# A different order of loads and of some twenty operations in the opening of a one-core attention and feed-forward kernel

## The chip, the cores and the metric

One core of a Trainium2 chip runs the program. The metric is the device time of one execution in microseconds (us); of several executions the median is taken.

## What is computed

Attention with a band and block summaries, then a feed-forward layer with a softmax-gated activation and a normalization. The reference, cut to what matters (4 batches, 8 heads, 768 positions, 64 wide; `d_model` 512, `d_ff` 1024):

```python
k_sum = k.reshape(B, H, nb, 32, D).max(axis=3)
v_sum = v.reshape(B, H, nb, 32, D).mean(axis=3)
scores_l = where(abs(i - j) < 16, scale * q @ k.T, -1e9)
scores_s = scale * q @ k_sum.T + log(32)
a = softmax(concatenate([scores_l, scores_s], -1))
x = a @ concatenate([v, v_sum])
h = x @ w_in
solu = h * softmax(h)
ln = (solu - mean) / sqrt(var + 1e-6) * g_ln
out = ln @ w_out
```

## The kernel before

**Tiling.** Queries are taken in groups of 256 positions (three per batch). For half of the heads of a group there is one round: `scores` (L671) multiplies queries with a window of 96 keys and 24 block maxima, VectorE (DVE) adds the mask and takes maxima, ScalarE (ACT) makes exponentials, a multiplication by the reciprocal sum follows (DVE or GpSimd, POOL), `values_turn` (L762) transposes the result on TensorE (PE), two copies bring it to SBUF, and `values` (L773) multiplies it with the value rows. The block means of `v` are rows 96 to 119 of that product: for batch 0 `mean_values_first` (L581) makes them on PE from three row blocks, for batch 1 `mean_values_pe` (L597) from three others. The result is split into a high and a low part (`xh`, `xl`), and `first` (L948) multiplies 128 rows with `w_in`, three matmuls per piece of weights (high by low, low by high, high by high). `solu` (L1023) does the gate and the normalization, `turn` (L1119) transposes, `second` (L1137) multiplies with `w_out`. Both weight matrices arrive as 64-bit words and are turned into two 32-bit parts by `rounded` (L487) and `split_w_in` or `split_w_out` (L522, L528): scale, sign bits, low word, shift, add, round (high part), subtract (low part), spread over ACT, DVE and POOL.

**Order.** Every call of `op` makes an operation that has a number, the engines that can run it, a planned cost and dependencies. `order` (L292) simulates a greedy schedule; `move` (L238) then takes each entry `(operation, engine, after)` of `MOVES` (L118), removes the operation from where it was and puts it behind the named one in that engine's line. `issue` (L210) emits the result: each engine runs its line in order. While PE's planned time is below `FILL` (L97), `keep_up` (L366) puts fillers, matmuls on zeros (L1346), ahead of the next PE operation.

**Loads.** Nearly all are issued by SyncE (SP, the queue's own rows are SPq) in one line; a few by ACT. Eight completion semaphores are used in turn by all loads, so a load is issued when the one eight places ahead of it has landed. In this text:

- w0 to w7 are the 512 KB pieces of `w_in` (w5 is operation 11), w8 to w15 those of `w_out` (w14 is 125, w15 is 126).
- r0, r1, r2 are the 512 KB value row blocks of batch 0 (12, 13, 14), r3, r4, r5 those of batch 1 (115, 116, 117).
- Q1 and Q2 are the 512 KB queries of the second and third group (Q2 is 136), V0, V1, V2 the 1024 KB value windows of the first three groups (V2 is 137).
- SP's order before: w0 k w1 w2 q k k k q w3 w4 w5 r0 r1 r2 V0 w6 w7 g Q1 V1 r3 w8 to w15 r4 r5 Q2 V2 and so on.
- ACT issues the broadcast of the block means into rows 96 to 119 of each value window of batch 0 (`load_v2`, L664): into V1 (114) and into V2 (242), each when that window has landed.

**PE's order in the opening.** Fillers; scores of group 0; 20 fillers; block means from r0 (32) and r1 (33); transpose (53); block means from r2 (34); transpose (73); values (56, 76); scores of group 1 (129); `first(0)` (138 to 145); scores (187); `first(1)` (195 to 202) with a transpose (179) and values (182) inside; block means from r3 and r4 (243); transpose (236); from r5 (244); `first(2)` begins (262); values (239); scores of group 2 (252), which read Q2; and so on.

Of the kernel before, what the change touches and what calls it, by code (L numbers as in the profile page):

```python
# [85 lines left out]
class Plan:  # L86
# [7 lines left out]
    SMALL, LATE = 40.0, 50.0  # L94
    LAND = 2.2
    START = 0.7
    COLD, FILL = 6.9, 21.6  # L97
    IDLE = 0.22
    WAIT, FAR = 1.5, 200
    DEAR = {"dve": 1.0, "act": 0.3, "pool": 1.0}  # L100
# [15 lines left out]


    MOVES = ((53, "pe", 33), (200, "pe", 199), (317, "pe", 327), (308, "pe", 317), (35, "act", 55), (77, "act", 109),  # L118
        (315, "act", 227), (296, "act", 240), (158, "act", 296), (214, "act", 301), (391, "act", 354),
        (247, "act", 380), (249, "act", 383), (526, "act", 446), (540, "act", 547), (602, "act", 582),  # L120
        (613, "act", 612), (664, "act", 668), (679, "act", 672), (1396, "act", 1196), (1875, "act", 1855),
        (102, "dve", 103), (146, "dve", 130), (175, "dve", 147), (171, "dve", 154), (223, "dve", 171),
        (203, "dve", 155), (210, "dve", 209), (297, "dve", 293), (314, "dve", 388), (322, "dve", 314),
        (371, "dve", 364), (527, "dve", 450), (452, "dve", 410), (445, "dve", 442), (419, "dve", 418),
        (663, "dve", 560), (706, "dve", 707), (678, "dve", 660), (869, "dve", 812), (1223, "dve", 1222),
        (1287, "dve", 1224), (1864, "dve", 1874), (97, "pool", 186), (99, "pool", 118), (250, "pool", 251),
        (170, "pool", 113), (233, "pool", 176), (234, "pool", 233), (298, "pool", 163), (213, "pool", 298),
        (420, "pool", 351), (606, "pool", 1150), (561, "pool", 606), (615, "pool", 585), (562, "pool", 615),
        (589, "pool", 588), (680, "pool", 1154), (814, "pool", 1300), (753, "pool", 1302), (909, "pool", 1303),)

    def __init__(self):
        self.ops, self.rings, self.banks, self.idle, self.slots = [], {}, {}, None, []
# [1259 lines left out]
```

## Time and profile before

| | |
|---|---|
| median of 3 runs | 356.59 us (355.8 to 357.35) |
| profiled execution | 356.37 us |
| its span, first to last instruction | 354.6 us |
| PE busy | 349.5 us, 99% |
| DVE, ACT, POOL busy | 294.7, 276.6, 167.2 us |
| chain that ended last | PE 93%, DMA 5% |

Times of rows are counted from the start of the span. Busy times overlap between engines. What the profile calls idle is the time an engine waited right before an instruction; behind the arrow stands what ended it. The DMA share can be a little above 1 because packets overlap.

### The profile page before, as it was taken

The page shows a single profiled execution, that of the slowest core. Times are in us where ns is not written, and L with a number is a line of the kernel's source. Part 1 is how long each engine was busy: PE and PEld are TensorE (multiplying, and loading weights), DVE is VectorE, ACT ScalarE, POOL GpSimd, SP SyncE. Part 2 cuts the span into 40 slices and gives each one's busy share as a digit, 9 for nine tenths or more (in the row PEclk, how much of TensorE's full clock was granted, in tenths as well). Part 3 has the DMA queues.
Part 4 walks back from the last instruction along what each step waited for, and adds up shares of the span by engine and source line. Part 5 has one row for each costly group of instructions (what it writes and reads, how often), then busy time and mean ns, then how long its engine had stood idle before and what let it go on. Part 6 is the DMA issues. An engine that isn't in the chain of part 4 may idle for free.

```text
span 354.6 us, 9335 instructions
## 1 busy us (share of the span) xinstructions
PE 349.5 (99%) x3312; PEld 275.4 (78%) x3312; DVE 294.7 (83%) x946; ACT 276.6 (78%) x810; POOL 167.2 (47%) x301
## 2 busy tenths in 40 slices
PE   8999999999999999999999999999999999999996
PEld 3528767878777887888888888888888888888886
DVE  3898999998999998996899998896897996947431
ACT  5777999997879979799796894994995996946310
POOL 6626425369777998307805445240335053533200
PEclk9999999999999999999999999999999999999999
DMA  7999996054525247267498382573443382344611
GB/s 250 412 408 408 352 411 227 35 129 156 179 84 190 95 150 259 82 212 255 144 284 288 93 274 99 168 259 132 152 153 136 97 283 63 126 142 169 216 61 59
DMA packets 28531, 68.19 MB, mean 192 GB/s; under 512 B 3853, under 2 KB 13325, under 8 KB 26949
## 3 DMA queue, kind: packets, MB, share of 16 engines
q1 hardware_dynamic: 24620, 60.87, 51.3%
q10 hardware_dynamic: 3864, 6.74, 5.3%
q8 instruction: 26, 0.43, 0.5%
q14 instruction: 21, 0.16, 0.1%
HBM read 49.55 MB, written 15.73 MB: 184 GB/s over the span
## 4 chain that ended last, share of the span: by engine, by line
PE 93%; DMA 5%; SPq 0%; ACT 0%; issue 0%; DVE 0%
PE o L1154 38%; PE h L959 13%; PE hu L978 13%; PE x L807 7%; PE hl L978 6%; PE hf L978 3%; DMA st_v<-in_vr 3%; PE s_0l L705 3%; PE s_1l L705 2%; DMA qt<-in_q 2%; PE t_0l L760 2%; PE t_1l L760 2%; PE vs_ps L591 2%; PE vs_ps1l L604 1%; PE x L799 1%; PE s_0r L705 0%
## 5 line engine op out<-in xcount | busy, mean ns | idle before, releaser
L1154 PE MATMUL o<-w,lh 128*128 128x512 f32 (+1 forms) x400 | 127.6, 385 | 0.0
L1154 PEld LDWEIGHTS o<-w,lh 128*128 128x128 f32 x400 | 74.1, 188 | 15.3 <-ACT at L405 0.2
L1154 PE MATMUL o<-w,ll 128*128 128x512 f32 (+1 forms) x200 | 76.2, 381 | 0.0
L732 ACT ACTIVATE e<-e,nm 128x120 f32<-128x120 f32 x192 | 73.4, 392 | 0.0
L959 PE MATMUL h<-w,xh 128*128 128x512 f32 x128 | 43.2, 401 | 0.0
L1154 PEld LDWEIGHTS o<-w,ll 128*128 128x128 f32 x200 | 37.6, 188 | 6.9
L732 ACT ACTIVATION_READ_ACCUMULATOR e<-e,nm 128x1 f32 x192 | 37.9, 197 | 0.0
L959 PEld LDWEIGHTS h<-w,xh 128*128 128x128 f32 x128 | 24.0, 188 | 6.7 <-ACT kw L405 0.8
L413 POOL TENSOR_TENSOR ll<-lt,lh 128x512 fp32r<-128x512 f32 x11 | 16.0, 1465 | 26.2 <-DVE lh L406 19.2
L633 POOL TENSOR_TENSOR st_v<-st_v 96x512 f32<-96x512 f32 (+3 forms) x28 | 23.9, 862 | 8.2 <-DMA st_v<-in_vb 7.7
L807 PEld LDWEIGHTS x<-at,vt 120*64 120x64 f32 (+1 forms) x768 | 24.4, 138 | 4.1 <-issue 2.0
L1061 ACT ACTIVATE he<-he,nmu 128x512 f32<-128x512 f32 x35 | 24.2, 722 | 4.0 <-DVE nmu L1052 3.6
L807 PE MATMUL x<-at,vt 120*64 120x64 f32 (+1 forms) x768 | 26.5, 224 | 0.0
L1064 ACT ACTIVATE sq<-he 128x1024 bf16<-128x1024 f32 x24 | 25.4, 1059 | 0.1
L1084 DVE STREAM_TRANSPOSE tbl<-he 128x1024 f32<-128x1024 f32 x18 | 22.3, 1239 | 3.9 <-ACT he L1061 2.3
L959 PE MATMUL h<-w,xl 128*128 128x512 f32 x64 | 25.0, 390 | 0.0
L1041 ACT ACTIVATE he<-hs,hm 128x512 f32<-128x512 f32 x24 | 17.2, 718 | 9.1 <-DVE hm L1031 9.1
L413 POOL TENSOR_TENSOR cv<-cv 128x512 int32<-128x512 int32 x8 | 11.0, 1378 | 26.2 <-ACT cv L509 13.3
L412 DVE TENSOR_TENSOR e<-e,z 128x960 f32<-128x960 f32 x18 | 22.2, 1232 | 0.1
L1160 ACT ACTIVATE os<-o,y 128x512 f32<-128x512 f32 x19 | 13.0, 685 | 11.7 <-PE o L1154 11.5
L413 POOL TENSOR_TENSOR xl<-sums,xh 128x256 fp32r<-128x256 f32 (+1 forms) x12 | 12.4, 1034 | 19.4 <-ACT xh L405 19.4
L412 DVE TENSOR_TENSOR ll<-lt,lh 128x512 fp32r<-128x512 f32 x25 | 19.7, 804 | 0.5 <-ACT lh L405 0.3
(250 smaller groups left out, 959.8 us busy)
## 6 DMA issues: line engine op xcount, KB each, us to landing
vt<-in_v SPq DMA_DIRECT2D x12, 1024.0 KB
farl<-tbl SPq DMA_DIRECT2D x18, 512.0 KB
lt<-farl SPq DMA_DIRECT2D x72, 128.0 KB
kraw<-in_k SPq DMA_DIRECT2D x16, 400.0 KB
out<-os ACTq DMA_DIRECT2D x23, 256.0 KB
qt<-in_q SPq DMA_DIRECT2D x11, 512.0 KB
raw<-in_w_in SPq DMA_DIRECT2D x8, 512.0 KB
raw<-in_w_out SPq DMA_DIRECT2D x8, 512.0 KB
```

Of the source, the lines that this page charges most:

```text
L412: by = {dve: lambda: nc.vector.tensor_tensor(out=to(), in0=a(), in1=b(), op=kind), pool: lambda: nc.gpsimd.tensor_tensor(out=to(), in0=a() ...
L413: pool: lambda: nc.gpsimd.tensor_tensor(out=to(), in0=a(), in1=b(), op=kind)}
L633: op(pool, 0.15 + w * 0.0021, lambda w=w, o=o: nc.gpsimd.tensor_tensor(out=o.ap[:n, :w], in0=x.ap[:n, :w], in1=x.ap[:n, w:2 * w], op=ALU.add),
L705: nc.tensor.matmul(sc.ap[j][cu * QT:(cu + 1) * QT, c:c + ks.shape[-1]], qs.ap[ds, 2 * pp + i, u * QT:(u + 1) * QT], ks, start=True, stop=True)
L732: nc.scalar.activation(out=e.ap[:, n, :], in_=e.ap[:, n, :], func=AF.Exp, bias=nm.ap[:, n:n + 1], scale=-1.0, accum_out=z.ap[:, n:n + 1])
L807: nc.tensor.matmul(xp()[j * D:(j + 1) * D, i, qs], vs.ap[:k, u, cs], at.ap[:k, u % 2, n[j] + u // 2, :], start=not apart, stop=not apart o ...
L959: nc.tensor.matmul(hp.ap, a.ap[:, c, ts], w.ap[:, i], start=(c == 0 and n == 0), stop=(c == NKC - 1 and n == 2))
L978: nc.tensor.matmul(to.ap, operand(y, n)[:, c], w(c).ap(i), start=first and c == 0 and k == 0, stop=c == 1 and k == 2, skip_group_check=True)
L1061: (act, 0.57, lambda sl=sl: nc.scalar.activation(out=e.ap[:, sl], in_=e.ap[:, sl], func=AF.Identity, bias=nmu.ap))], port=True)
L1064: op(act, 1.13, lambda: nc.scalar.activation(out=sq.ap, in_=e.ap, func=AF.Square, accum_out=ss.ap), r=[e], w=[sq, ss])
L1084: op(dve, 1.13, lambda: nc.vector.transpose(out=tb.ap.rearrange("p (q c a) -> p q c a", q=4, a=32), in_=of().rearrange("p (c q a) -> p q c ...
L1154: nc.tensor.matmul(o.ap[:, cols], a.ap[:, f, :], w.ap[:, i, cols], start=(f == 0 and n == 0), stop=(f == NFC - 1 and n == 2))
```

## The change

Eighteen entries of `MOVES` are new or other, and `FILL` goes from 21.6 to 20.6, with which 15 fillers stand ahead of operation 32, not 20. No operation is added or removed.

- **SP:** w5 (11) goes behind r1, so r0 and r1 are ahead of it. r4 and r5 (116, 117) go behind w13, ahead of w14 and w15. V2 (137) goes behind w15, which puts it ahead of Q2 (136).
- **POOL:** the adding for w10 (226) comes from DVE, one half of the centring of `solu(0)` (156) from ACT, one sum of weights (456) from DVE. The order there is now: w5's low part (99), the keys' copy for scores 252 (250), ..., w9's add (176), 226, 156, the maxima's copy for 252 (251), w11's add (233); before, 251 and 250 stood behind 99.
- **ACT:** the low word of w9 (174) moves behind the two exponentials of `solu(0)` (149, 150); the scaling of w15 (365) ahead of the second half of one round's exponentials (320).
- **DVE:** the second half of `xl` of group 0 (78) moves ahead of two steps of w7; the maximum of `solu(0)` (148) ahead of w9's shift (175); the mean of `solu(0)` (155) and a maximum of `solu(1)` (203) behind two steps of w10; w11's low part (235) ahead of three steps of `solu(1)`; w15's low word (367) comes from ACT.

```diff
-    COLD, FILL = 6.9, 21.6
+    COLD, FILL = 6.9, 20.6
...
-        (315, "act", 227), (296, "act", 240), (158, "act", 296), (214, "act", 301), (391, "act", 354),
-        (247, "act", 380), (249, "act", 383), (526, "act", 446), (540, "act", 547), (602, "act", 582),
-        (613, "act", 612), (664, "act", 668), (679, "act", 672), (1396, "act", 1196), (1875, "act", 1855),
-        (102, "dve", 103), (146, "dve", 130), (175, "dve", 147), (171, "dve", 154), (223, "dve", 171),
-        (203, "dve", 155), (210, "dve", 209), (297, "dve", 293), (314, "dve", 388), (322, "dve", 314),
...
-        (1287, "dve", 1224), (1864, "dve", 1874), (97, "pool", 186), (99, "pool", 118), (250, "pool", 251),
-        (170, "pool", 113), (233, "pool", 176), (234, "pool", 233), (298, "pool", 163), (213, "pool", 298),
-        (420, "pool", 351), (606, "pool", 1150), (561, "pool", 606), (615, "pool", 585), (562, "pool", 615),
-        (589, "pool", 588), (680, "pool", 1154), (814, "pool", 1300), (753, "pool", 1302), (909, "pool", 1303),)
+        (174, "act", 150), (315, "act", 227), (296, "act", 240), (158, "act", 296), (214, "act", 301),
+        (365, "act", 358), (391, "act", 354), (247, "act", 380), (249, "act", 383), (526, "act", 446),
+        (540, "act", 547), (602, "act", 582), (613, "act", 612), (664, "act", 668), (679, "act", 672),
+        (1396, "act", 1196), (1875, "act", 1855), (102, "dve", 103), (78, "dve", 106), (146, "dve", 130),
+        (148, "dve", 147), (175, "dve", 148), (171, "dve", 154), (223, "dve", 171), (155, "dve", 225),
+        (203, "dve", 155), (210, "dve", 209), (297, "dve", 293), (235, "dve", 297), (367, "dve", 366),
...
+        (99, "pool", 118), (250, "pool", 99), (170, "pool", 113), (226, "pool", 176), (156, "pool", 226),
+        (251, "pool", 156), (233, "pool", 251), (234, "pool", 233), (298, "pool", 163), (213, "pool", 298),
+        (420, "pool", 351), (456, "pool", 352), (606, "pool", 1150), (561, "pool", 606), (615, "pool", 585),
...
+        (909, "pool", 1303), (11, "sp", 13), (116, "sp", 124), (117, "sp", 116), (137, "sp", 126),)
```

## Rows read from the trace of the kernel before

**Rows 1.** The page: busy us, share of the span, instructions.
```profile
PE 349.5 (99%) x3312; PEld 275.4 (78%) x3312; DVE 294.7 (83%) x946; ACT 276.6 (78%) x810; POOL 167.2 (47%) x301
```

**Rows 2.** All waits of PE: us in total, times, longest.
```profile
PE vs_ps L1346 <- DVE zero L430: 1.0, 1, 1.0
PE vs_ps L591 <- DMA st_v<-in_vr: 0.7, 1, 0.7
```

**Rows 3.** The chain that ended last: start us, us, what.
```profile
9.78 10.31 DMA st_v<-in_vr
...
20.23 3.59 PE vs_ps L591 x8
...
28.95 0.43 PE x L799 x4
...
42.00 1.59 PE h L959 x6
...
46.26 1.00 PE vs_ps1l L604 x8
...
50.84 0.24 PE s_0l L705
```

**Rows 4.** Timeline of PE: start us, us, instruction, count, [idle before it].
```profile
15.03 4.49 PE L1346 MATMUL vs_ps<-zero 128*128 128x512 bf16 x20
20.23 3.59 PE L591 MATMUL vs_ps<-st_v,sel 128*24 128x512 f32 x8 [0.72 <-DMA st_v<-in_vr]
```

**Rows 5.** Timeline of SP's queue: issues, each started by an earlier load's landing.
```profile
17.41 0.33 SPq L655 DMA_DIRECT2D qt<-in_q  x1
...
20.11 0.33 SPq L661 DMA_DIRECT2D vt<-in_v  x1
21.39 0.33 SPq L579 DMA_DIRECT2D st_v<-in_vr  x1
22.65 11.79 SPq L484 DMA_DIRECT2D raw<-in_w_out  x8
...
26.41 0.33 SPq L484 DMA_DIRECT2D raw<-in_w_out  x1
...
47.31 0.33 SPq L562 DMA_DIRECT2D kraw<-in_k  x1
```

**Rows 6.** Timeline of ACT.
```profile
22.21 0.67 ACT L496 ACTIVATE cv<-raw 128x512 f32<-128x512 f32 x1
...
26.91 0.68 ACT L496 ACTIVATE cv<-raw 128x512 f32<-128x512 f32 x1
27.61 0.59 ACT L405 COPY at<-t_1l 120x512 f32<-120x512 f32 x1
...
51.13 0.81 ACTq L667 DMA_DIRECT2D vt<-vsum  x1
```

**Rows 7.** Timeline of DVE.
```profile
20.97 1.15 DVE L412 TENSOR_TENSOR e<-e,z 128x960 f32<-128x960 f32 x1
...
40.59 0.75 DVE L1049 SCALAR_TENSOR_TENSOR he<-h,hz,he 128x512 f32<-128x512 f32 x1
...
44.92 0.69 DVE L412 CUSTOM_DVE_ANT_0 cv<-cv 128x1024 uint16<-128x1024 uint16 x1
45.76 1.16 DVE L412 TENSOR_TENSOR e<-e,z 128x960 f32<-128x960 f32 x1
```

**Rows 8.** Timeline of POOL.
```profile
40.58 1.29 POOL L413 TENSOR_TENSOR cv<-cv 128x512 int32<-128x512 int32 x1
50.99 1.29 POOL L413 TENSOR_TENSOR cv<-cv 128x512 int32<-128x512 int32 x1 [9.12 <-DVE hz L1044]
...
57.43 1.12 POOL L1057 TENSOR_SCALAR he<-he,nmu 128x512 f32<-128x512 f32 x1
```

**Rows 9.** Busy us per stretch (PE, PEld, DVE, ACT, POOL), PEclk, DMA share, GB/s.
```profile
30.00:35.00 5.00, 5.00 (x67) 4.11 (x64) 4.72 (x22) 2.90 (x7) 3.42 (x4) 1.00 1.03 411
35.00:40.00 5.00, 5.00 (x50) 3.90 (x49) 4.92 (x25) 4.97 (x23) 2.23 (x4) 1.00 1.03 305
```

More of the change, by code (lines that the diff above doesn't have):

```diff
@@ L123 @@
-        (203, "dve", 155), (210, "dve", 209), (297, "dve", 293), (314, "dve", 388), (322, "dve", 314),
-        (371, "dve", 364), (527, "dve", 450), (452, "dve", 410), (445, "dve", 442), (419, "dve", 418),
-        (663, "dve", 560), (706, "dve", 707), (678, "dve", 660), (869, "dve", 812), (1223, "dve", 1222),
-        (1287, "dve", 1224), (1864, "dve", 1874), (97, "pool", 186), (99, "pool", 118), (250, "pool", 251),
-        (170, "pool", 113), (233, "pool", 176), (234, "pool", 233), (298, "pool", 163), (213, "pool", 298),
@@ new lines @@
+        (1396, "act", 1196), (1875, "act", 1855), (102, "dve", 103), (78, "dve", 106), (146, "dve", 130),
+        (148, "dve", 147), (175, "dve", 148), (171, "dve", 154), (223, "dve", 171), (155, "dve", 225),
+        (203, "dve", 155), (210, "dve", 209), (297, "dve", 293), (235, "dve", 297), (367, "dve", 366),
+        (314, "dve", 388), (322, "dve", 314), (371, "dve", 364), (527, "dve", 450), (452, "dve", 410),
+        (445, "dve", 442), (419, "dve", 418), (663, "dve", 560), (706, "dve", 707), (678, "dve", 660),
@@ new lines @@
+        (869, "dve", 812), (1223, "dve", 1222), (1287, "dve", 1224), (1864, "dve", 1874), (97, "pool", 186),
+        (99, "pool", 118), (250, "pool", 99), (170, "pool", 113), (226, "pool", 176), (156, "pool", 226),
+        (251, "pool", 156), (233, "pool", 251), (234, "pool", 233), (298, "pool", 163), (213, "pool", 298),
+        (420, "pool", 351), (456, "pool", 352), (606, "pool", 1150), (561, "pool", 606), (615, "pool", 585),
+        (562, "pool", 615), (589, "pool", 588), (680, "pool", 1154), (814, "pool", 1300), (753, "pool", 1302),
```

## The prediction

> **What bounds the kernel now.** The page comes first: PE is busy 349.5 us of a 354.6 us span [rows 1]. Next I asked for every wait of PE: there are two in the whole program, 1.0 us at the very start and 0.7 us for the first value block [rows 2]. From 20.23 us to the end PE never stands idle. So no edit behind 20.23 us can gain anything by itself. What can be gained is in the chain's opening [rows 3]: PE runs 20 fillers from 15.03 to 19.52, idles 0.72, and begins the block means at 20.23, when r0 lands [rows 4]. From there any lead is kept only as long as nothing that PE needs is late for it, and everything that was just in time before is late by as much as PE is early. The third view is therefore the loads. SP's queue gives landings: each of its issues waits for the load eight earlier [rows 5]. 17.41 is the landing of w5, 20.11 of r0, 21.39 of r1, 22.65 of r2, 26.41 of w6, 47.31 of r5. Blocks of 512 KB land 1.26 to 1.28 us apart, in the order of issue; only between w5 and r0 it is 2.7, so one delay of 1.4 us lies there. DMA share is 1.03 in both stretches of [rows 9], so the loads have no gaps to close: a load that is put forward pushes another back by its size.
>
> **The change part by part.**
>
> *Fillers and r0.* r0 takes w5's place and lands at 17.41 instead of 20.11. Fifteen fillers at 4.49/20 = 0.2245 us end at 15.03 + 3.37 = 18.40 [rows 4]. They, and no longer the load, set the start of operation 32: 18.42 instead of 20.23, a lead of 1.81 us. It is the largest that this change can make. r1 takes r0's place, 20.11; PE wants it at 18.42 + 3.59/2 = 20.22 [rows 4]. No wait.
>
> *w5* takes r1's place, 21.39. ACT begins to scale it at 22.21 [rows 6], behind exponentials that don't depend on PE's lead. Cost nothing; the cover is 0.8 us.
>
> *What the lead meets next.* The transpose (53) would begin at 18.42 + 3.59 = 22.01, but its input is multiplied until 20.97 + 1.15 = 22.12 [rows 7]: 0.15 lost, lead 1.65. r2 lands at 22.65, as before, while that transpose runs. The second values operation (76) stands at 28.95 [rows 3] and would begin at 27.30. It needs the copy that ACT begins at 27.61 and ends 28.20, behind the scaling of w6 at 26.91 [rows 6], which can't begin before w6 lands at 26.41. So that pair moves by 0.5 at most, and 76 begins at about 27.75: lead 1.2. `first(1)` begins its second half at 42.00 [rows 3] in a bank that DVE gives free at 40.59 + 0.75 = 41.34 [rows 7]. Moved by nothing, this leaves 0.6 of lead; moved by as much as PE, 1.2. Operations 78 and 148 go forward here and take DVE steps for w7 and w9 out of the way; I take the middle, 0.95.
>
> *The other moves.* They spare what limits the lead later. The multiplication that the next transpose needs ends at 45.76 + 1.16 = 46.92, and the transpose comes at 46.26 + 1.00 = 47.26 [rows 3, 7]: only 0.34 of slack. Taking 226 off DVE frees 0.69 [rows 7], and setting 155 and 203 later doesn't delay it, since they stay ahead of it. On POOL 226 costs 1.29 and 156 up to 1.12 [rows 8]. Behind them wait 251 and 233, and for 226 ACT's rounding of w10, for 156 the squares of `solu(0)`. POOL does nothing between 40.58 + 1.29 = 41.87 and 50.99 in this trace [rows 8], so 2.4 us fit without anybody waiting; without that cover it would be 2.4 us on scores 252, which read the copy 251. 250 goes ahead of 251 only: nothing. ACT loses 156 and 367; DVE takes the latter. 174, 365, 175 and 235 change places with neighbours whose results PE takes later: nothing, with at most one operation (0.7 us, as the scalings of [rows 6]) on either side. 456 runs when PE is in `second`, on an engine busy 47% [rows 1]: nothing.
>
> *r4 and r5.* r5 lands at 47.31, and its matmuls follow those of r3 and r4, which end at 46.26 + 1.00 = 47.26, and one transpose [rows 3, 5]: a slack smaller than the lead. r4 landed a block earlier, at about 46.0 by an estimate from these rows, for 46.26. Both now go two places forward, 2.5 us earlier, and that wait doesn't arise. w14 and w15 come 2.5 us later. w14 now takes r4's turn in the semaphores, in which it waits for ACT's first broadcast to land; the queue has blocks in flight then, as before. Both weights are used by ACT and DVE far behind this.
>
> *V2 ahead of Q2.* This is the step that I think decides. Before, Q2 followed r5: an estimate from 47.31 and one block, 48.6; V2 two blocks later, 51.1, which agrees with ACT's broadcast into V2 at 51.13 [rows 6]. Now w15 takes the 47.31, V2 lands at 49.85 and Q2 at 51.1, since the bytes ahead of it are the same sum. Scores 252 read Q2 and begin at 50.84 in this trace [rows 3]. They needed it 2.2 us after it landed; now it lands behind their old start. PE begins r0's matmuls 0.12 after the landing [rows 4, 5], so 252 begins at 51.22: the lead of 0.95 is gone, and 0.38 with it. For ACT, which comes to the broadcast when V2 has landed, the step is a gain; PE is in order and nothing of it can pass 252.
>
> *Sum.* +1.81 - 0.15 - 0.45 - 0.25 at the stations above makes 0.95 in hand at 252, then a wait of about 1.35: the end comes 0.4 us later. DVE and ACT have their work for the stretch behind 252 done earlier than before, so nothing is lost twice, and PE, which never waited there [rows 2], can't win it back. The profiled execution would take 356.37 + 0.4 = 356.8. It was 0.22 below the median of the runs; on their footing the forecast is **357.0 us**. Bounds of the unknown: the delay of 1.4 us seen between w5 and r0 may fall otherwise. Once less ahead of Q2, it lands at 49.7 and the result is 355.6; once more, 52.5 and 358.4. Neither end is nearer by a row, since the total of bytes is the same; I keep the middle.
>
> **The rivals.** *Q2 comes in time.* If Q2 lands by 49.9, the lead of 0.95 (0.6 to 1.2) reaches the end: 356.59 - 0.95 = 355.6. Against it: three successive blocks in [rows 5] land in issue order and evenly spaced, and a block behind 1024 KB has to wait for these bytes. For it: the delay of 1.4 us may fall elsewhere, and the chance of that is a quarter. The Trainium skill, DMA: Bandwidth & Descriptors, section Queues, rings and completion order, says that completion is not first in, first out per issuing engine, as each of the engines that share a load finishes by itself. By that rule Q2 could be complete with V2 at 49.85 and the time would be this rival's; the landings seen here keep their order.
>
> *Everything fits.* No station takes anything and Q2 is early: 1.81 gained, 354.8. [rows 6, 7] speak against it, since 22.12 and 26.41 are not PE's to move. 0.05.
>
> *Slower: the broadcast falls on Q2.* With V2 landed at 49.85, ACT can issue the second broadcast about 1 us earlier than 51.13 [rows 6], while Q2's last bytes move. Place: DMA engines between 50 and 52. Price: in the stretch with the first broadcast they moved 305 GB/s where the one before had 411 [rows 9]; 5 us by 106 GB/s is 530 KB, or 1.3 us. Q2 would land at 52.4, 252 begin at 52.5, and the result be 356.59 + 1.7 = 358.3. Any landing of Q2 after 50.84 - 0.12 = 50.7 ends later than before; after 52.5 the loss is over 1.8 us. Against it: the loss in [rows 9] comes in the stretch that begins some us after an issue, not at once. 0.12. The same page and section says that a DMA engine goes round the queues it has work for, packet by packet, which is this sharing; the fall in [rows 9] agrees.
>
> A rival in which the lines come out otherwise than they are written is left out: each engine runs the line that `move` made.
>
> **How the numbers follow.** Forecast (Q2 waited for, within 0.5 us of 51.1) 0.58, Q2 in time 0.25, everything fits 0.05, broadcast on Q2 0.12. What a measurement of this kernel can tell from no change is 0.5%, 1.8 us. The forecast and the first rival lie inside it with all of their bounds but small tails; everything fits sits on its edge, the slower rival just inside. Faster 0.06, same 0.86, slower 0.08. The range from 355.2 to 358.3 takes in the first rival with 0.4 below it for the scatter of the runs, and the slower rival's value.
>
> **What the profile would show.** Right: 15 fillers and `vs_ps` at 18.4 without an idle row; a new wait of PE for `qt<-in_q` of 1 to 1.5 us at `s_0l`, which begins near 51.2; the matmuls on r3 to r5 without a wait; PE's rows behind 52 us about 0.4 later than now. Wrong: `s_0l` before 50.5 without a wait, or new waits of PE for ACT or POOL between 27 and 50 beyond 1 us in sum, or a first wait behind 52 us.

## The result, and the profile after

The changed kernel takes 358.45 us (median of 9 runs, 357.31 to 359.22), the kernel before 356.5 us in the same measurement (9 runs): the ratio is 1.0054, with an interval of 1.0042 to 1.0067. It is slower by 1.9 us (1.5 to 2.4 by the interval), a little more than the 1.8 us that the prediction took as the least these runs can tell from no change, and just above the forecast range, which ended at 358.3. The profiled execution took 359.14 us with a span of 357.4.

The page, beside [rows 1]: instructions of each engine and their busy time.

```profile
PE 349.7 (98%) x3307; PEld 274.9 (77%) x3307; DVE 296.8 (83%) x945; ACT 276.2 (77%) x808; POOL 172.3 (48%) x304
```

PE is busy 349.7 us, for 349.5 before, in a span that is 2.8 us longer, so the loss is idle time of PE. DVE is 2.1 us busier although it gave two operations away and took one; how that can be is the heart of this case: rows that are longer than their work. All waits of PE, beside the two of [rows 2] (us in total, times, longest):

```profile
PE vs_ps L1349 <- DVE zero L433: 1.0, 1, 1.0
PE t_0l L763 <- POOL e L416: 0.8, 1, 0.8
PE s_0l L708 <- DMA qt<-in_q: 0.7, 1, 0.7
PE s_0l L708 <- POOL ss L1071: 0.4, 1, 0.4
PE t_1l L763 <- DVE e L415: 0.4, 1, 0.4
PE x L802 <- ACT at L408: 0.3, 1, 0.3
PE t_0l L763 <- DVE e L415: 0.3, 1, 0.3
PE o L1157 <- DVE w L537: 0.2, 1, 0.2
```

The wait for r0 is gone, the forecast wait for `qt` is there, and six others are new. The timeline of PE, beside [rows 4], shows where they stand (start us, us, instruction; of groups of matmuls the first row):

```profile
15.30 3.41 PE L1349 MATMUL vs_ps<-zero 128*128 128x512 bf16 x15
18.64 3.61 PE L594 MATMUL vs_ps<-st_v,sel 128*24 128x512 f32 x8
22.54 0.24 PE L763 MATMUL t_0l<-ident,e 64*120 64x64 f32 x1 [0.28 <-DVE e L415]
...
47.30 0.24 PE L763 MATMUL t_1l<-ident,e 64*120 64x64 f32 x1 [0.38 <-DVE e L415]
...
51.61 0.28 PE L708 MATMUL s_0l<-kw,qt 64*64 64x120 f32 x1 [0.65 <-DMA qt<-in_q]
...
72.63 0.50 PE L1157 MATMUL o<-w,lh 128*128 128x512 f32 x1 [0.17 <-DVE w L537]
...
74.03 0.39 PE L708 MATMUL s_0l<-kw,qt 64*64 64x120 f32 x2 [0.44 <-POOL ss L1071]
...
133.83 0.27 PE L763 MATMUL t_0l<-ident,e 64*120 64x64 f32 x1 [0.80 <-POOL e L416]
```

Setting the start of the same matmul after against before gives PE's lead or lateness along the program (worked out from the two timelines; minus is a lead):

```
first scores        11.03 -> 11.30   +0.27   (the loads of this execution land later)
block means (32)    20.23 -> 18.64   -1.59
transpose (53)      23.76 -> 22.54   -1.22
values (76)         28.78 -> 28.05   -0.74
first(1)            41.93 -> 41.60   -0.33
transpose t_1l      47.19 -> 47.30   +0.11
scores 252          50.77 -> 51.61   +0.84
output weights w15  71.57 -> 72.63   +1.06
scores behind it    72.48 -> 74.42   +1.95
transpose t_0l     131.12 -> 133.83  +2.71
last matmul's end  351.35 -> 354.11  +2.76
```

So the lead of 1.6 us is won and eaten up as far as 47 us, Q2 costs 0.73 (from 0.11 late to 0.84), the stretch from 71 to 75 us another 1.1, and the one near 131 another 0.8. The forecast's sum has nothing for the last two.

**What stands behind them.** Near 70 us, DVE in the kernel before (first fence) and after it (second), and then POOL in both:

```profile
69.18 1.45 DVE L534 SCALAR_TENSOR_TENSOR w<-cv,g_sb,w 128x512 fp32r<-128x512 f32 x2
70.55 0.68 DVE L816 TENSOR_TENSOR xl<-x,xh 128x512 fp32r<-128x512 f32 x1
```

```profile
69.37 0.70 DVE L537 SCALAR_TENSOR_TENSOR w<-cv,g_sb,w 128x512 fp32r<-128x512 f32 x1
70.28 2.29 DVE L537 SCALAR_TENSOR_TENSOR w<-cv,g_sb,w 128x512 fp32r<-128x512 f32 x1 [0.21 <-ACT w L534]
72.50 0.68 DVE L819 TENSOR_TENSOR xl<-x,xh 128x512 fp32r<-128x512 f32 x1
73.10 0.67 DVE L1135 TENSOR_TENSOR ll<-lt1l,lh 128x512 fp32r<-128x512 f32 x1
73.69 0.68 DVE L1135 TENSOR_TENSOR ll<-lt1r,lh 128x512 fp32r<-128x512 f32 x1
```

```profile
70.04 2.23 POOL L413 TENSOR_TENSOR e<-e,z 128x960 f32<-128x960 f32 x1
```

```profile
70.24 1.79 POOL L416 TENSOR_TENSOR e<-e,z 128x960 f32<-128x960 f32 x1
```

The two steps of DVE are the last ones of w14 (operation 364) and w15 (371). Before, 371 is running when POOL comes to its multiplication: DVE's two steps end at 69.18 + 1.45 = 70.63, and POOL's row is the long one, 2.23. After, POOL begins at 70.24, 0.04 ahead of 371, its row takes 1.79, and that of 371 takes 2.29 in place of about 0.75 (1.45 for the two steps before): it ends at 72.57, which is 0.54 behind POOL's end at 72.03. Whichever engine begins first keeps its usual duration, and the other's row is drawn out until the first has ended. The step itself had waited for ACT's rounding of w15 (370), which begins at 69.52 and not at 69.00: ACT stands 0.44 us ahead of it, behind its two small stores of sums, the second of which begins at 68.77 here and at 67.65 before. ACT before and after:

```profile
69.00 0.72 ACT L531 ACTIVATE w<-cv,g_sb 128x512 fp32r<-128x512 f32 x1 [0.28 <-POOL cv L413]
```

```profile
68.77 0.70 ACTq L620 DMA_DIRECT2D vsum<-vs  x1
69.52 0.72 ACT L534 ACTIVATE w<-cv,g_sb 128x512 fp32r<-128x512 f32 x1 [0.44 <-issue]
```

What follows is in order on DVE, so the halves of `ll` end 1.9 us later than before, at 74.37, and PE's second score matmul begins 0.05 behind that. (The wait is put down to POOL's small `ss`, which only happened to end last before it: in the kernel before, these scores begin at 72.35 and that `ss` at 73.28.)

Near 131 us it is one of DVE's sums of weights, `w1s`, before and after:

```profile
125.64 0.68 DVE L412 TENSOR_TENSOR w1s<-ws_own,w1s 128x512 fp32r<-128x512 f32 x1
```

```profile
128.11 2.49 DVE L415 TENSOR_TENSOR w1s<-ws_own,w1s 128x512 fp32r<-128x512 f32 x1
```

DVE's maxima behind it come late, POOL waits 1.34 us for them ahead of its multiplication of `e`, and PE 0.80 for that.

### The profile page after: what moved, and what is told of

Its sections match the earlier page's. It is cut to its first block, busy times and chain, and to the rows that moved or that the text cites. A ratio compares the mean times of both kernels' runs of the same rounds, so it can differ in the third digit from the quotient of the medians.

```text
span 357.4 us, 9326 instructions
## 1 busy us (share of the span) xinstructions
PE 349.7 (98%) x3307; PEld 274.9 (77%) x3307; DVE 296.8 (83%) x945; ACT 276.2 (77%) x808; POOL 172.3 (48%) x304
## 4 chain that ended last, share of the span: by engine, by line
PE 74%; DMA 10%; DVE 8%; ACT 5%; POOL 1%; issue 1%; ACTq 0%; SPq 0%
PE o L1157 33%; PE hu L981 13%; PE hl L981 6%; DMA qt<-in_q 5%; PE x L810 5%; PE h L962 5%; DMA raw<-in_w_in 5%; PE hf L981 3%; PE s_0l L708 2%; PE s_1l L708 2%; PE t_0l L763 2%; DVE e L727 1%; PE t_1l L763 1%; DVE hm L1039 1%; POOL e L416 1%
## 5 line engine op out<-in xcount | busy, mean ns | idle before, releaser
L735 ACT ACTIVATION_READ_ACCUMULATOR e<-e,nm 128x1 f32 x192 | 37.1, 193 | 0.0
L416 POOL TENSOR_TENSOR cv<-cv 128x512 int32<-128x512 int32 x9 | 12.7, 1416 | 23.0 <-ACT cv L512 7.6
```

The source lines that it names most:

```text
L416: pool: lambda: nc.gpsimd.tensor_tensor(out=to(), in0=a(), in1=b(), op=kind)}
L735: nc.scalar.activation(out=e.ap[:, n, :], in_=e.ap[:, n, :], func=AF.Exp, bias=nm.ap[:, n:n + 1], scale=-1.0, accum_out=z.ap[:, n:n + 1])
```

## The experiments

All were timed against the kernel before on the same chip. The edits are entries of the list of moved operations: (operation, engine, the operation it goes behind).

### One place undone at a time, and all three

The theory: three places lose time independently, Q2 behind V2, the steps for w15 (365, 367), and the sum of weights 456 on POOL. The rival: one of them sets all, and its undoing brings everything back.

Q2 ahead of V2 again:

```diff
-    (137, "sp", 126)
```

> The changed kernel with Q2 ahead of V2, as before. Three-places theory (each of the three stalls behind 50 us, Q2 0.8 us, operations on DVE and POOL that shut each other out near 70 us 1.0 us and near 128 us 0.8 us, has a cause of its own): PE's wait for Q2 goes, the lead at the scores of group 2 is 0.2 to 0.6 us, the two later stalls stay; 357.2 to 357.6 us. One-cause theory (the later stalls only follow from PE's shift by Q2): all three go; 355.8 to 356.4 us. Third possibility: ACT's broadcast waits for V2 instead, near 51 us, and takes the lead away again; 356.6 to 357.2 us with no PE wait before 60 us.

Measured: 357.97 us, ratio 1.0037 (1.0027 to 1.0048), above the 357.2 to 357.6 expected. No wait for `qt`; PE still has 0.18 us of lead at w15, is 0.71 late behind it and 1.43 late near 132. About 0.6 us of the 1.9 is Q2's.

The two steps for w15 back in their old places:

```diff
-    (365, "act", 358)
-    (367, "dve", 366)
```

> The changed kernel with the two steps of w15 (365, 367) as before. Three-places theory: ACT's rounding of w15 is no longer issued behind its small stores, DVE's subtraction for w15 begins ahead of POOL's multiplication and takes 0.7 to 0.8 us, not 2.3; the waits of PE at 72 and 74 us go; 357.3 to 357.6 us. One-cause theory: no difference to the changed kernel, 358.2 to 358.6 us.

Measured: 356.76 us, ratio 1.000 (0.999 to 1.001): the whole slowdown in the medians, and less time than the 357.3 to 357.6 expected. Its profile has no wait near 72 to 74 any more. The wait of 0.8 us near 131 for POOL's `e` stays, and that for Q2 is absent in this one execution, whose first scores begin 0.66 us earlier than in the profile of before; so it says less of Q2 than e1 does.

456 back on DVE:

```diff
-    (456, "pool", 352)
```

> The changed kernel with the weight sum 456 on DVE as before. If 456 on POOL is what sets POOL ahead of DVE near 128 us: the wait of PE for POOL near 133 us (0.8 us) goes; 357.5 to 357.8 us. If that stall comes from PE's shift alone: 358.2 to 358.6 us.

Measured: 357.78 us, ratio 1.0033 (1.0022 to 1.0045). The wait near 131 is gone and the other two stay: PE is 0.79 late at 51.56, 1.89 at 74.37, and ends 1.94 late (353.29 for 351.35).

All three undone:

```diff
-    (365, "act", 358)
-    (367, "dve", 366)
-    (456, "pool", 352)
-    (137, "sp", 126)
```

> The changed kernel with 137, 365, 367 and 456 as before. Three-places theory: all stalls behind 50 us go and the lead of the opening (0.2 to 0.6 us at the scores of group 2) is kept; 355.8 to 356.3 us, faster than before by 0.2 to 0.7 us. One-cause theory: the same as without 137 alone. Third possibility (ACT's broadcast waits for V2): 356.4 to 357.0 us.

Measured: 355.88 us, ratio 0.9979 (0.9969 to 0.999): faster than the kernel before. No single place sets all of it. The three undone singly give 0.6, 1.9 and 0.75 us by the ratios, 3.3 in sum, and together 2.7; in the profile after PE loses 2.6 at the three (0.73 from 47 to 51 us, 1.11 from 51 to 75, 0.76 near 131). Each interval is 0.4 us to either side and a gain is the difference of two, so the split is known to about 0.6 us. Why the two steps for w15 give 1.9 here, and 1.1 in the trace and by themselves below, is open.

### One part done alone, on the kernel before

V2 ahead of Q2, with the entry of the changed kernel:

```diff
+    (137, "sp", 126)
```

> The kernel before with one move alone: V2 is loaded ahead of Q2. PE has no lead here (20 fillers, r0 as before), so whatever Q2 is late is paid in full. Theory of the late Q2: Q2 lands a block behind its old place, near 51.1 to 51.3, scores 252 begin at 51.2 to 51.5 instead of 50.84 behind a new wait of PE for qt of 0.4 to 0.7 us, and the end comes 0.4 to 0.7 us later, 357.0 to 357.3. Rival, Q2's place only costs together with the other moves (the landing is hidden when nothing else is shifted): no wait for qt, 356.6.

Measured: 358.68 us, ratio 1.0057 (1.0043 to 1.0071). Neither theory had this. A wait of PE tells why:

```profile
PE vs_ps1l L604 <- DMA st_v<-in_vr: 1.2, 1, 1.2
```

Operation 126 is w15. In the kernel before, w15 stands ahead of r4 and r5, so the entry put V2's 1024 KB ahead of these two as well, and PE waited 1.2 us for a value block: it is 1.69 late at once and 1.52 at the end. Behind that, PE comes to scores 252 at 52.48 and doesn't wait for Q2. This measures another edit than was meant: a block of values that is late in this stretch is paid almost in full.

The edit that was meant:

```diff
+    (137, "sp", 117)
```

> The kernel before with V2 ahead of Q2 and behind r5, as these two stand in the changed kernel; r4 and r5 keep their places here. PE has no lead. Theory of the late Q2: Q2 lands near 51.1 instead of 48.6, scores 252 begin at 51.2 to 51.6 instead of 50.84 behind a wait of PE for qt of 0.3 to 0.7 us, no wait for a value block (r5 stands as before), and the end comes 0.4 to 0.7 us later, 356.9 to 357.2. Rival: the shift of PE alone is enough to bring on the collision of DVE's 371 with POOL's multiplication near 70; 371 then takes 2.3 us and the time is 358 or more. Second rival: Q2's place costs nothing without the lead, 356.5.

Measured: 356.8 us, ratio 1.0004 (0.9991 to 1.0017), with the expected wait:

```profile
51.04 0.28 PE L705 MATMUL s_0l<-kw,qt 64*64 64x120 f32 x1 [0.50 <-DMA qt<-in_q]
```

The scores begin at 51.04 for 50.77, 371 begins ahead of POOL and takes its usual time, and PE ends 0.52 us later. Only 0.07 of that is there behind 72 us; the rest comes with a wait of 0.23 at 165.42 for POOL's `xl`, behind a sum of `st_v` whose load lands later than in the trace of before. The medians show 0.1 us with 0.5 to either side, which holds both 0.4 and 0. PE comes to the scores 0.31 ahead in this execution, so it is Q2's landing that sets their start: Q2's place costs 0.3 us there, and whatever lead PE has. Alone it doesn't bring on the collision.

The two steps for w15 alone:

```diff
+    (365, "act", 358)
+    (367, "dve", 366)
```

> The kernel before with the two moves for w15 alone: 365 goes behind 358 on ACT and 367 from ACT to DVE. Theory A, the moves by themselves put the rounding of w15 (370) so late that POOL's multiplication of e begins ahead of DVE's operation 371: 371 takes about 2.3 us instead of 0.83, the scores behind it wait, and the end comes 1.0 to 1.9 us later, 357.6 to 358.5. Theory B, the collision needs the other moves as well, which shift PE and POOL by some tenths; alone, 371 still begins first and takes 0.7 to 0.85 us, POOL's row is the long one (2.2), and the time stays at 356.6 (within 0.4).

Measured: 357.64 us, ratio 1.0031 (1.0019 to 1.0044). DVE and then POOL:

```profile
69.60 2.29 DVE L534 SCALAR_TENSOR_TENSOR w<-cv,g_sb,w 128x512 fp32r<-128x512 f32 x1 [0.22 <-ACT w L531]
```

```profile
69.55 1.79 POOL L413 TENSOR_TENSOR e<-e,z 128x960 f32<-128x960 f32 x1
```

Theory A holds: with everything else as before, the two moves turn the order of the two rows round by themselves, and the same 2.29 us appears. PE waits 0.45 for w15 and 0.53 behind it and ends 1.25 us later.

456 alone:

```diff
+    (456, "pool", 352)
```

> The kernel before with operation 456 alone moved from DVE to POOL. Theory of the shared port: POOL's short rows near 124 to 127 come later behind the extra 1.3 us, DVE's two sums near 125 (ws_v and w1s) then begin while POOL holds the port, and w1s takes 2.0 to 2.5 us instead of 0.68; DVE's maxima and hm come 1 to 2 us late, POOL's multiplication of e begins after 130.5 instead of 129.22, and PE waits 0.4 to 0.8 us for it at t_0l near 131: 356.9 to 357.2. Rival: the wait near 133 needs the lateness that the other two places give; alone, 456 on POOL is hidden, no wait of PE over 0.2 us there, and the time stays at 356.5 (within 0.3).

Measured: 356.95 us, ratio 1.0016 (1.0001 to 1.003). Of the waits of PE the one that matters here, then DVE's two sums and POOL's rows beside them:

```profile
PE t_0l L760 <- POOL e L413: 0.8, 1, 0.8
```

```profile
124.35 1.30 DVE L412 TENSOR_TENSOR ws_v<-ws_own,ws_v 128x512 fp32r<-128x512 f32 x1
125.58 2.48 DVE L412 TENSOR_TENSOR w1s<-ws_own,w1s 128x512 fp32r<-128x512 f32 x1
127.97 0.68 DVE L1036 TENSOR_REDUCE hm<-h 128x1 f32<-128x512 f32 x1
```

```profile
125.01 1.24 POOL L413 TENSOR_TENSOR xl<-sums,xh 128x256 fp32r<-128x256 f32 x1
126.21 1.29 POOL L413 TENSOR_TENSOR ws_own<-w,ws_own 128x512 f32<-128x512 f32 x1
127.58 0.51 POOL L1068 TENSOR_SCALAR ss<-ss 128x1 f32<-128x1 f32 x1
129.44 1.79 POOL L413 TENSOR_TENSOR e<-e,z 128x960 f32<-128x960 f32 x1 [1.34 <-DVE hm L1038]
```

In the kernel before, the same two sums begin first, at 125.03 and 125.64, and take 0.69 and 0.68 us; the row that is drawn out there is POOL's sum of `st_v`, 1.20 us for 0.73. Here `w1s` comes to stand behind two of POOL's rows in turn, ends at 128.06, 0.56 behind the second, and holds the maxima of DVE back; POOL then idles 1.34 us for them ahead of its multiplication of `e`, for which PE waits. The operation that was moved is not the one that is late: it made POOL's later rows fall on DVE's sums. POOL's multiplication begins at 129.44 and not behind 130.5 as expected, since PE is 0.69 ahead in this execution until then; the wait turns that into 0.17 late. What PE loses further on (it ends 0.64 late) comes at 165 us, with the late load that is in the trace of V2 behind r5 too, and isn't 456's.

The early loads and the 15 fillers alone, without any of the moved operations:

```diff
-    COLD, FILL = 6.9, 21.6
+    COLD, FILL = 6.9, 20.6
...
+    (11, "sp", 13), (116, "sp", 124), (117, "sp", 116)
```

> The kernel before with the early loads alone: r0 and r1 ahead of w5, r4 and r5 two places forward, 15 fillers; none of the dozen operations moves. Theory: operation 32 begins at 18.3 to 18.6 instead of 20.23 with a lead of 1.6 to 1.9 us, and the same stations take from it: the copy for the second values operation (near 27.6), the bank at 41.3, and e for the transpose, ready at 46.9 as before, so that the lead behind 47 is 0.2 to 0.5 us; nothing collides behind it, and the time is 0.2 to 0.5 us under that of before, 356.0 to 356.3. That makes the moved operations together worth nothing or a few tenths. Rival 1: the operations moved on DVE near 28 to 47 are what lets the lead pass; without them PE waits more there and the time is 356.6 or more. Rival 2: the whole lead arrives, 354.8.

Measured: 356.69 us, ratio 0.9998 (0.9985 to 1.0011): rival 1. The lead is 1.22 at the block means (r0 lands late in this execution, and PE waits 0.54 us for it) and 0.83 near 28, and then PE waits 0.95 us in `first` for DVE's `xl` at 33.72 and is 0.33 late. The version with three places undone has the same loads and no such wait, so the moves that it keeps (78 and 148 among them) carry the lead past 33 us; which of them does is open. The loads without them are worth nothing that these runs can tell.

### The rule of the shared path, and what 226 costs

If DVE is only shut out when it reads two operands from SBUF, then operations with one operand in a PSUM bank must run at their usual speed beside POOL. In the changed kernel 371 is put two steps later, behind `xl` and the first half of `ll`, which read a bank each:

```diff
-    (371, "dve", 364)
+    (371, "dve", 355)
```

> The changed kernel with operation 371 (DVE's last step for w15) three steps later on DVE, behind xl and the first half of ll, each of which reads one operand from a PSUM bank. Theory of the shared port (rows of DVE and POOL with two operands in SBUF exclude each other, whoever begins first holds): xl and ll take their usual 0.68 us while POOL multiplies e, and 371 ends 0.6 to 0.75 us behind the end of POOL's row, whenever it begins, so its row is 0.7 to 1.4 us long and not 2.29. Then the second half of ll is done at 73.4 instead of 74.37, PE's wait of 0.44 us at the scores of 74.03 goes, and the end comes 0.2 to 0.6 us earlier than that of the changed kernel: ratio to before about 1.004. Rival, DVE is slowed by any work of POOL: xl and ll take 1.2 us or more beside POOL's row, 371 comes later than 73.5, and the time stays or grows. Rival, 371 is slow by itself: 2.3 us again wherever it stands.

Measured: 357.48 us, ratio 1.0025 (1.0016 to 1.0034). DVE and POOL:

```profile
69.79 0.69 DVE L819 TENSOR_TENSOR xl<-x,xh 128x512 fp32r<-128x512 f32 x1
70.57 0.69 DVE L1135 TENSOR_TENSOR ll<-lt1l,lh 128x512 fp32r<-128x512 f32 x1
71.18 1.20 DVE L537 SCALAR_TENSOR_TENSOR w<-cv,g_sb,w 128x512 fp32r<-128x512 f32 x1
72.30 0.68 DVE L1135 TENSOR_TENSOR ll<-lt1r,lh 128x512 fp32r<-128x512 f32 x1
```

```profile
70.04 1.79 POOL L416 TENSOR_TENSOR e<-e,z 128x960 f32<-128x960 f32 x1
```

`xl` and `ll` take 0.69 us each under POOL's row; 371 comes later, is shorter, and ends at 72.38, again 0.55 behind POOL's end (71.83). Both rivals fall: DVE isn't slowed by any work of POOL, and 371 isn't slow by itself. PE's wait at the scores is gone. The gain by the medians, 1.0 us against the changed kernel's 358.45, is more than the 0.2 to 0.6 expected; its last matmul ends 1.2 us earlier than after, of which the wait of 0.44 and the split of the two score halves (74.42 - 74.03) explain 0.8; another 0.2 is there from the scores 252 on, for which Q2 lands earlier in that execution (51.40 for 51.61).

The Trainium skill, SBUF — State Buffer, section Who interferes with whom, says that a DVE instruction with two SBUF inputs contends with a GpSimd instruction that reads SBUF, that one with at most one such input doesn't (outside the modes that use two ports), and that the lock is exclusive and issue order decides who blocks. The rows of after, e6, e11 and e14 agree with each of the three, with 2.29, 1.79 and 0.69 us.

226 on POOL has the same mark: beside its row (44.84 for 1.29 us in the kernel after) DVE's multiplication 193 takes 1.94 us and not the 1.16 of [rows 7]. Both rows of the kernel after:

```profile
45.21 1.94 DVE L415 TENSOR_TENSOR e<-e,z 128x960 f32<-128x960 f32 x1
```

```profile
44.84 1.29 POOL L416 TENSOR_TENSOR cv<-cv 128x512 int32<-128x512 int32 x1 [2.88 <-DVE nmu L1055]
```

To see whether this holds PE's lead, 226 goes back to DVE, on the version with three places undone:

```diff
-    (226, "pool", 176), (156, "pool", 226)
+    (156, "pool", 176)
```

> The version with three places undone (without V2 ahead of Q2, without the two moves for w15, without 456 on POOL), and with 226 back on DVE as well; 156 stays on POOL. If the row of POOL is what stretches DVE's multiplication of e near 45 (1.94 us instead of 1.16), that row is back at 1.16. Theory 1: nothing is won by it, since 226 takes its 0.69 us on DVE ahead of the multiplication again, e is ready at 46.9 to 47.1 in both, PE's wait for it near 47.2 stays at 0.3 to 0.5 us, and the time stays within 0.3 us of 355.9. Theory 2: the stretched row is what keeps PE's lead from passing there; the wait falls under 0.15 us and the time to 355.4 or less.

Measured: 355.89 us, ratio 0.9985 (0.9973 to 0.9997). DVE:

```profile
44.48 0.83 DVE L414 CUSTOM_DVE_ANT_0 cv<-cv 128x1024 uint16<-128x1024 uint16 x1
45.23 0.19 DVE L740 RECIPROCAL z<-z 128x8 f32<-128x8 f32 x1
45.46 1.16 DVE L414 TENSOR_TENSOR e<-e,z 128x960 f32<-128x960 f32 x1
```

Theory 1: the row is back at 1.16 and nothing is won, since 226 takes 0.83 ahead of it. `e` is ready at 46.62 and PE still waits 0.35 for it. That is no gain over the version with three places undone, where `e` is ready at 47.08, since this whole execution runs earlier: counted from the start of DVE's maximum two or three rows ahead (43.88 and 44.32), `e` is ready after 2.74 us here and 2.76 there. What 226's move saves on DVE, POOL's row takes back.

### A version that is meant to be better

On top of that version (with 226 back), two of the waits left in its trace are taken away:

```diff
-    (203, "dve", 155)
+    (203, "dve", 193)
...
+    (74, "act", 35)
```

> The version with 226 back on DVE (355.89 at its own measurement), with two more operations moved off the waits that are left in its trace: ACT's copy of the transposed e (74) goes ahead of the scaling of w6, which waits 1.1 us for its load while the copy's input is ready; DVE's maximum over a bank (203) goes behind the multiplication of e (193) that the transpose near 46.8 waits for. Theory: the lead of PE is held at these two waits (0.4 us near 27.6, 0.3 us near 46.8), both go or shrink under 0.15 us, the lead behind 47 grows from 0.4 to 0.8 to 1.1 us, and the end comes 0.3 to 0.7 us earlier, 355.2 to 355.6. Rival: something behind it takes the lead back (Q2 near 50, or a collision of DVE and POOL that the shift of PE brings on), and the time stays at 355.9 or grows by up to 1 us.

Measured: 355.93 us, ratio 0.9985 (0.9972 to 0.9997), the same as without. Both waits are gone, and the lead from 47 to 57 us is 0.79, for 0.42 in the version it starts from. But a new wait of 0.33 us for POOL's `e` at 40.32 takes what the first edit had won, 0.39 us go between 57 and 58, and PE ends 0.48 ahead of before, against 0.63 without the two edits. (In this execution the block means begin at 18.70, behind a wait of 0.20 for r0, and at 18.29 in the other, so the two ends compare only roughly.) The rival holds by the medians: something behind takes the lead back. Which operation does so near 57 us is open. The version with three places undone, at 355.88 us, beats both kernels and was not bettered.

## Why the prediction was wrong

**Fillers and r0**: right. 15 fillers, then the block means at 18.64 without idle time, a lead of 1.59 (forecast 1.81). The loads of this execution land 0.27 later; with Q2 first, where the first scores begin as before, it is 1.85. The delay of 1.4 us that stood between w5 and r0 isn't tied to a place: in the kernel after, r0 lands at 17.77 and r1 at 20.30; with the early loads alone, r0 lands at 18.89, 2.6 behind the load ahead of it.

**What the lead meets next**: the three stations are right, the losses a little short. The lead falls by 0.37 to the transpose (forecast 0.15), by 0.48 to the second values operation (0.45) and by 0.41 to `first(1)` (0.25), so 0.33 is left of it, not 0.95. (The middle of 0.6 and 1.2, which the forecast took there, is 0.9.)

**V2 ahead of Q2**: right. A wait of 0.65 us for `qt`, the scores at 51.61 (forecast 51.22), PE late by 0.84 and not by 0.4. The wait is shorter than the 1.35 forecast, because the lead was gone by then, and the scores come 0.39 later because all loads do: w15 lands at 47.70 here, for the 47.31 of the forecast. The completion counts in the trace show the order: V2 is whole at 50.20 and Q2 at 51.48. Its sixteen parts end one by one, the first at 48.91, ahead of the last of V2, but the last 1.28 us behind it; so the rival "Q2 in time" falls. The rival of the broadcast that falls on Q2 has its condition missing: ACT issues it at 51.24, behind other work, and not 1 us earlier than the 51.13 of [rows 6].

**"2.4 us fit without anybody waiting"**, of 226 and 156 on POOL: this failed. POOL was idle, but its row is not free for DVE: 193 became 1.94 us long, so "taking 226 off DVE frees 0.69" came to nothing, and PE went from 0.33 ahead to 0.11 late at this transpose. But POOL's row isn't what cost the lead: with 226 back on DVE, `e` is no earlier. There the wait went when DVE's maximum 203 was put behind 193; the forecast had let 203 pass since it "stays ahead" of the multiplication.

**365 and 367, at "nothing" or at most one operation of 0.7 us**: this failed, and cost most. The step looked at who takes the results of these operations, not at what their new times do to the order of DVE's next step and POOL's next row. One such exchange is worth most of the other engine's row of 1.79 us: 2.29 in place of 0.75.

**456 at "nothing", as POOL is busy 47%**: this failed in the same way, for 0.76 us of PE's time in the trace. POOL's share says that its own queue has room, and nothing of what its rows do to DVE's.

**Sum and range.** On the footing of profiled executions the forecast was 356.8, and 359.14 was measured. It lacked these two places, 1.11 and 0.76 us, and had 0.44 too little at Q2: 2.31 of the 2.34 us that are missing. No rival and no bound had two engines shutting each other out, though the trace of before has such rows: POOL's 2.23 us for a multiplication that takes 1.79 elsewhere, and DVE's 1.01 us for a step on one column that takes 0.15. The program has it too: `order` adds to the planned cost of an operation that is marked `port` what is left of the other engine's row (`lock`, `held`), but `move` puts an operation elsewhere with its plain cost, and nothing is planned again behind it. So an entry of `MOVES` can bring on a collision that the plan had avoided. The sign that was named as "a first wait behind 52 us" is what came.

## What to carry to other kernels

When work goes from DVE to POOL, list what DVE does while POOL's rows run: operations with two operands in SBUF wait for the end of POOL's row or make it wait, and `xl` and `ll`, which read a PSUM bank, don't. Two durations of one form of operation in one trace (1.79 and 2.23 before, 0.70 and 2.29 after) are the mark of it; the wait sits inside the row, so it counts as busy time and the idle columns don't show it. A move that shifts anything by some tenths must be held against every such pair that begins within that distance.

## What the runs showed of the hardware that was not expected

The row that is shut out ends 0.53 to 0.56 us behind the other's end in five places (371 after, in e6 and in e11, `w1s` in e14, 226 in e9), which is some 0.15 us less than such a step takes alone (0.68 to 0.75). What is done of it while it is shut out, the runs don't show. POOL is shut out just as well with an operation on one column: `ss` on 128x1 takes 0.51 us behind `w1s` in e14, for 0.19 usually. And a collision can run through several rows: the 2.48 us of `w1s` spans the ends of two rows of POOL, which follow each other without giving DVE a turn. It isn't always so: at 46.1 us in the kernel after, 193 gets its turn between two rows of POOL, and the second of these (46.12) takes 1.60 us for its usual 0.7. What decides between the two is open.
